# A decode layer, forward and backward: score rows by chunk quarter, outers from score rows, pipelined emission, weights turned on VectorE

## Chip, core and metric

One NeuronCore of a Trainium2 chip runs the whole program. The metric is device time in microseconds (us), lower is better. The kernel before was timed three times on its own: median 883.74 us, from 881.05 to 886.12.

## What is computed

A layer for decoding (two batches, one new token each) and its gradients. Out of the reference:

```python
def _A_ref(x, k_cache, v_cache, wq, wo):          # B=2, Sq=1, D=576, Hq=32, Hkv=16, Sk=4096, Dh=128
    q = (x @ wq).reshape(B, Sq, Hq, Dh).transpose(0, 2, 1, 3)
    k = jnp.repeat(k_cache, 2, axis=1); v = jnp.repeat(v_cache, 2, axis=1)
    p = _softmax(jnp.einsum("bhqd,bhkd->bhqk", q, k) * Dh ** -0.5)
    o = jnp.einsum("bhqk,bhkd->bhqd", p, v)
    return o.transpose(0, 2, 1, 3).reshape(B, Sq, Hq * Dh) @ wo
def _B_ref(x, w_gate, w_up, w_down):              # F=4608
    return jnp.einsum("bsf,fd->bsd", (x @ w_gate) * (x @ w_up), w_down)
out = x + _A_ref(layernorm(x), ...) + _B_ref(layernorm(x), ...)
```

The outputs are this sum and its vector-Jacobian product with grad_out for x, both caches and all five weights. The gradients of the caches have the shape of the caches; each is an outer product of a row over the 4096 tokens with a row of 128. All data are bf16. Reads and writes are about 92.5 MB each, 67.1 MB of each being caches.

## The kernel before

The program is written with a framework that places the semaphores and gives each tile a slot of its tag (`bufs` slots each); it also orders each engine's instructions by readiness and by the order in which they are written, so that later code can run ahead. Each engine runs its own queue in that order. Loads are issued on SyncE's queue, stores on GpSimd's.

There are four groups of four key/value heads (eight query heads each). `group_front` (L322) loads a group's wq and wo, makes q and, with the vector-transposed wo and the stationary Wdy, the gradient of the attention output, and spreads both over partitions (`rep`). `attention` (L377) runs for each batch: GpSimd writes W[0] and W[1], zero-filled stationaries with the query or gradient at eight columns of each 32 (L382), and dM (L386), from which TensorE and ScalarE make BD, block-diagonal rows (L395, L398). Then K scores: each of four heads is loaded as 128 partitions by 32 chunks of 128, turned in 32x32 blocks of bf16 pairs by VectorE (L100 for every vector transpose), and eight matmuls of 512 columns (L414) add into one score tile of 128x1024 fp32. Of its rows, 4 blocks of 32 tokens by 32, only 8 in each 32 hold heads. The softmax over it takes the maximum through TensorE (L467 to L478), the exponential (L481), the sum through TensorE (L484) and the probabilities, which are turned (pT). `token_rows` (L441) turns pT on TensorE into rows by token (L446). The same score code runs on V; then L498 to L511 make the score gradients. `contract` (L424) multiplies with V or K (L430, outputs of 32 partitions in turn); `outer` (L451) makes the 4096x128 gradients by matmuls with 32 rows (L458) into ps_o, a tile of two PSUM banks with two slots, which `evac` (L81) copies out on VectorE (L88) or ScalarE (L91), whichever its running tally finds less loaded. One store of 1 MB follows four evacuations (L462).

`mlp_slice` (L231) handles 512 of the 4608 hidden columns, after each attention and once more at the end: gate and up products with the weights as stationary and two columns moving (L249), the down weights turned on VectorE (L259), the gate/up weights turned on TensorE (`transposed`, L220: L226, L227) and multiplied (L283), rows turned (L291, L296), and outers with two rows (`outer_flat` L201: L212; L308, L315). `group_back` (L522) does the same for wq and wo (L226, L531, L538, L212, L551). The score tile has one slot; caches and weights share ten slots of tag nat, output staging three of tag st.

## Time and profile before

| | |
|---|---|
| median of three runs | 883.74 us |
| the profiled execution, and its span | 885.2 us, 883.4 us |
| TensorE, VectorE, ScalarE, GpSimd busy | 692.2, 390.3, 364.7, 110.1 us |
| mean granted TensorE clock | 0.621 of 2.4 GHz |
| moved by DMA | 185.90 MB, 210 GB/s on average |

The span is the time from the first to the last instruction on the core. A group of instructions is one line, operation and shape; its mean is that of one instruction, and matmuls overlap, so that the busy time divided by the count is often less. The idle time behind the second bar is the time in which the engine stood just before instructions of the group, with what ended it. The DMA share is the mean over the 16 DMA engines. A granted clock of 0.50 is the 1.2 GHz level, 1.00 the 2.4 GHz level; between them is a mixture of both.

### The profile page before, as it was taken

To read this page: it belongs to the slowest core of one execution; us is meant where nothing else is said; L and a number is where in the kernel's file an instruction comes from. 1 tells how busy PE (TensorE), PEld (TensorE's weight loads), DVE (VectorE), ACT (ScalarE), POOL (GpSimd) and SP (SyncE) were. 2 spreads that over 40 slices of the span, in tenths; PEclk is the share of its full clock that TensorE was granted. 3 is DMA by queue.
4 is the path that set the end of the run, shared out by engine and by line. 5 is a ranking of instruction groups with operands and counts; after the bars stand their busy time and mean duration, and the time that the engine had idled before them with its cause. 6 is when DMAs were issued, how large, how long until landed. Compare 5 with 4: busy or idle time off the path is not lost. (4 is left out here: it accounts for less than half of the span.)

```text
span 883.4 us, 14680 instructions
## 1 busy us (share of the span) xinstructions
PE 692.2 (78%) x6469; PEld 338.6 (38%) x6469; DVE 390.3 (44%) x439; ACT 364.7 (41%) x395; POOL 110.1 (12%) x211
## 2 busy tenths in 40 slices
PE   4686878679866897689868687977986689768995
PEld 3244324444333432344424332444433343234552
DVE  8640555145561356244454055514556135624344
ACT  1055425543126531744305551554312653174332
POOL 3010110111201110111111011011120111011111
PEclk9885559555685557755579555855558555775555
DMA  9459623993309850896315972399430985084322
GB/s 338 161 195 401 249 81 115 419 362 136 108 1 391 326 182 25 310 419 247 110 52 185 406 252 81 114 419 363 135 107 1 382 338 180 24 288 185 140 99 89
DMA packets 52368, 185.90 MB, mean 210 GB/s; under 512 B 3880, under 2 KB 18352, under 8 KB 44112
## 3 DMA queue, kind: packets, MB, share of 16 engines
q1 hardware_dynamic: 28064, 92.49, 28.1%
q0 software_dynamic: 24240, 92.48, 27.5%
q8 instruction: 50, 0.82, 0.4%
q14 instruction: 14, 0.11, 0.0%
HBM read 92.48 MB, written 92.48 MB: 209 GB/s over the span
## 5 line engine op out<-in xcount | busy, mean ns | idle before, releaser
L91 ACT CAST so<-ps_o 128x1024 bf16<-128x1024 f32 x221 | 215.9, 1020 | 148.3 <-PE ps_o L458 92.5
L458 PE MATMUL ps_o<-BD,r 32*128 32x512 bf16 x512 | 130.9, 531 | 83.6 <-ACT so L91 49.4
L414 PE MATMUL ps_sc<-X,W 128*128 128x512 bf16 x512 | 170.8, 488 | 15.0 <-POOL W L382 9.7
L100 DVE STREAM_TRANSPOSE X<-kv 128x2048 f32<-128x2048 f32 x64 | 146.8, 2303 | 51.2 <-PE ps_sc L414 51.0
L462 POOL DMA_DIRECT2D out_dram<-so x64 | 48.4, 756 | 409.5 <-ACT so L91 377.4
L414 PEld LDWEIGHTS <-W 128*128 128x128 bf16 x512 | 56.3, 117 | 111.9 <-issue 74.3
L458 PEld LDWEIGHTS <-r 32*128 32x128 bf16 x512 | 27.8, 96 | 126.6 <-issue 97.4
L88 DVE CAST so<-ps_o 128x1024 bf16<-128x1024 f32 x35 | 43.0, 1229 | 27.2 <-PE ps_o L458 17.9
L226 PE MATMUL ps_o<-ident,wgu 128*128 128x128 bf16 x288 | 44.2, 308 | 5.8 <-DVE so L88 4.7
L518 DVE TENSOR_SCALAR oT<-ps_m 128x8 bf16<-128x8 f32 x8 | 1.4, 170 | 104.5 <-PE ps_m L437 104.5
L481 ACT ACTIVATE ex<-ps_sc,negb 128x1024 f32<-128x1024 f32 x8 | 8.9, 1114 | 89.9 <-DVE negb L478 89.9
L430 PE MATMUL ps_m<-kv,dsT 128*32 128x128 bf16 x1024 | 38.9, 267 | 0.9 <-issue 0.9
L91 ACT COPY wT<-ps_o 128x1152 bf16<-128x1152 bf16 x21 | 23.5, 1120 | 35.1 <-PE ps_o L227 35.1
L315 PE MATMUL ps_o<-rows,xn_bf 2*128 2x512 bf16 x72 | 36.5, 614 | 1.0 <-DVE stw L88 0.8
L88 DVE CAST stw<-ps_o 128x1024 bf16<-128x1024 f32 x18 | 21.9, 1218 | 33.8 <-PE ps_o L315 26.1
L91 ACT COPY r<-ps_m 128x1024 bf16<-128x1024 bf16 x16 | 16.5, 1034 | 44.3 <-PE ps_m L446 44.3
L91 ACT CAST stw<-ps_o 128x1024 bf16<-128x1024 f32 x18 | 18.0, 1013 | 37.5 <-PE ps_o L315 37.5
L430 PEld LDWEIGHTS <-dsT 128*32 128x32 bf16 x1024 | 21.5, 111 | 25.8 <-issue 25.8
L226 PEld LDWEIGHTS <-wgu 128*128 128x128 bf16 x288 | 25.9, 136 | 14.1 <-issue 10.5
L91 ACT CAST std<-ps_o 128x1024 bf16<-128x1024 f32 (+1 forms) x27 | 20.7, 801 | 23.2 <-PE ps_o L212 23.1
L100 DVE STREAM_TRANSPOSE Xd<-wd 128x1152 f32<-128x1152 f32 x9 | 12.4, 1377 | 39.9 <-DMA wd<-in_B_w_down_dram 39.9
L382 POOL COPY W<-rep 32x32 bf16<-32x32 bf16 x64 | 13.2, 207 | 104.2 <-PE ps_sc L414 101.4
(165 smaller groups left out, 846.0 us busy)
## 6 DMA issues: line engine op xcount, KB each, us to landing
out_dram<-so POOLq DMA_DIRECT2D x64, 1024.0 KB, 9.8
kv<-in_A_k_cache_dram SPq DMA_DIRECT2D x32, 1024.0 KB, 14.2
kv<-in_A_v_cache_dram SPq DMA_DIRECT2D x32, 1024.0 KB, 8.0
out_dram<-stw POOLq DMA_DIRECT2D x18, 512.0 KB, 3.4
wd<-in_B_w_down_dram SPq DMA_DIRECT2D x9, 576.0 KB, 7.1
out_dram<-std POOLq DMA_DIRECT2D x9, 576.0 KB, 3.1
wo<-in_A_wo_dram SPq DMA_DIRECT2D x4, 1152.0 KB, 19.3
wgu<-in_B_w_gate_dram SPq DMA_DIRECT2D x9, 512.0 KB, 3.8
```

The costliest lines, as they stand in the source:

```text
L88: nc.vector.tensor_copy(out=out, in_=in_)
L91: nc.scalar.copy(out, in_)
L100: nc.vector.transpose(out, in_)
L226: nc.tensor.transpose(tp[:, k - k0, dc * P:(dc + 1) * P], src(k, dc), ident[:])
L315: nc.tensor.matmul(o[:, k, :], lhsT=xn_bf[0:2, (dc + k) * P:(dc + k + 1) * P], rhs=rows[0:2, 1 + w, :], start=True, stop=True)
L382: nc.gpsimd.tensor_copy(view(W[t][:], 32 * a, 32, 32 * a, [[G * P, 4], [P + 2, G], [1, 2]]), view(rep[:], 32 * a, 32, t * 4 * GH * 2 + b, ...
L414: nc.tensor.matmul(s_ps[:, half, :], lhsT=Wt[:, be, l, :], rhs=view(X[:], 0, P, half * 16 * Dh + 64 * (be // 2) + be % 2, [[Dh, 16], [2, 3 ...
L430: nc.tensor.matmul(o_ps[32 * q:32 * q + 32, l, :], lhsT=rowsT[:, c, :], rhs=heads[l][:, c, :], start=(c < 4), stop=(c >= NCH - 4))
L458: nc.tensor.matmul(o[:, q % 2, :], lhsT=r2[32 * q:32 * q + 32, c // 4, :], rhs=bd[32 * q:32 * q + 32].rearrange("p l d -> p (l d)"), start ...
L462: nc.gpsimd.dma_start(oview[b, :, G * g:G * g + G, 8 * Dh * s:8 * Dh * (s + 1)], so[:].rearrange("p l c d -> p l (c d)"))
L481: nc.scalar.activation(ex[:], s_ps[:].rearrange("p a n -> p (a n)"), AF.Exp, bias=negb[:], scale=SCALE, accum_out=z[:])
L518: nc.vector.tensor_scalar(oT[:, 1, :, b], dq_ps[:], SCALE, None, op0=ALU.mult)
```

## The change

- A head's scores take 16 matmuls of 256 columns in place of 8 of 512. W has 24 more columns, and a view shifted by 8 columns puts the chunk quarter cq into the row, so that the score tile is 128x256, with all rows in use and two slots.
- The K/V outers take the score rows themselves (pr, ds) as stationaries; BD gets four copies, each masked on GpSimd to one quarter. `token_rows` is gone. A unit of outers makes two ps_o tiles from four matmuls; a store writes 256 KB of one head and one token block.
- `contract` works per head, with its own evacuation of 128 columns.
- The order is written by hand: `fill` puts two units of outers and some units of the MLP or of the last group's back part (`side`) behind each head's scores.
- wq, gate and up are turned on VectorE (Xq, Xw) and multiplied in `dxn`, which adds into accx; gate and up products have x as stationary and the weights moving. The MLP and group outers take 32-row operands (xnr, dyr, hb, R) in four or two row blocks.
- nat has 11 slots, st 4.

The diff, cut to its core:

```diff
--- before
+++ after
         return ps.tile(list(shape), dtype, tag="m", bufs=2, name="ps_m")
 
     def ps_sc():
-        return ps.tile([P, 2, 512], FP32, tag="sc", bufs=1, name="ps_sc")
-
-    def ps_o(shape=(P, 2, 512), dtype=FP32):
-        return ps.tile(list(shape), dtype, tag="o", bufs=2, name="ps_o")
+        return ps.tile([P, 256], FP32, tag="sc", bufs=2, name="ps_sc")
+
+    def ps_o():
+        return ps.tile([P, 2, 512], FP32, tag="o", bufs=2, name="ps_o")
...
-        return sb.tile(list(shape), BF16, tag="nat", bufs=10, name=name)
+        return sb.tile(list(shape), BF16, tag="nat", bufs=11, name=name)
...
-        return sb.tile(list(shape), BF16, tag="st", bufs=3, name=name)
+        return sb.tile(list(shape), BF16, tag="st", bufs=4, name=name)
...
-    def transposed(src, tail, n, dst):
...
-    def mlp_slice(i):
...
+    def stationaries(rep, half):
+
...
+        nc.vector.tensor_tensor(
+            view(Wm[:], 0, P, 0, [[8, 32], [2, 4], [1, 2]]), view(rep, 0, P, 0, [[2, 32], [0, 4], [1, 2]]),
+            view(mask8[:], 0, P, 0, [[0, 32], [2, 4], [1, 2]]), ALU.mult)
+        for h in range(2):
+            off, dims = half(h)
+            n = len(dims) > 1 and dims[0][1] or 1
+            nc.gpsimd.tensor_copy(
+                view(Wt[:], 64 * h, 64, 0, [[P // n, n], [1, P // n]]), view(Wm[:], 64 * h, 64, off, dims))
...
+    def dxn(Wm, Wt, X, pos, xoff, xstep):
+
+        dp = ps_m([P, 160])
+        for s in range(8):
+            for q in range(4):
+                nc.tensor.matmul(dp[32 * q:32 * q + 32, 0:P], lhsT=view(Wm[:], 0, P, 8 * pos(q, s), [[1, 32]]),
+                                 rhs=view(X[:], 0, P, xoff(q, s), [[xstep, 4], [2, 32]]),
+                                 start=(s == 0), stop=(s == 7))
+        for s in range(4):
+            for q in range(4):
+                nc.tensor.matmul(dp[32 * q:32 * q + 32, P:160], lhsT=view(Wt[:], 0, P, 8 * (4 * q + s), [[1, 32]]),
+                                 rhs=view(X[:], 0, P, 8 * FS + (2 * q + s // 2) * 64 + s % 2, [[2, 32]]),
+                                 start=(s == 0), stop=(s == 3))
+        nc.vector.tensor_add(accx[:], accx[:], dp[:])
...
+        def gate_up():
+            wgu = m["wgu"]
+            ug = ps_m([P, 2, P])
+            for w in range(2):
+                for dc in range(5):
+                    k = 4 * w + dc if dc < 4 else 8
+                    for a in range(4):
+                        nc.tensor.matmul(ug[32 * a:32 * a + 32, 1 - w, :], lhsT=xs[:, dc if dc < 4 else 4 + w, :],
+                                         rhs=wgu[:, k, P * a:P * (a + 1)], start=(dc == 0), stop=(dc == 4))
...
+        def back():
+            wgu = m["wgu"]
+            Xw = xtile([P, 9, FS], "Xw")
+            t32(pairs(Xw[:].rearrange("p c n -> p (c n)")), pairs(wgu[:].rearrange("p c n -> p (c n)")))
...
+        def outer_gu(w):
+            def f():
+                hb = m["hb"]
+                if w == 0:
+                    m["st"] = stile([P, 8, FS], "stw")
+                st = m["st"]
+                o = [ps_o(), ps_o()]
                 for dc in range(4):
+                    for a in range(4):
+                        nc.tensor.matmul(o[a // 2][:, a % 2, dc * P:(dc + 1) * P],
+                                         lhsT=xnr[32 * a:32 * a + 32, dc * P:(dc + 1) * P],
+                                         rhs=hb[32 * a:32 * a + 32, 1 + w, :], start=True, stop=True)
+                for A in range(2):
+                    evac(view(st[:], 0, P, 4 * w * FS + 256 * A, [[P, 2], [FS, 4], [1, P]]),
+                         o[A][:].rearrange("p a (d f) -> p a d f", d=4), 1024)
...
+                for k in range(2):
+                    for aa in range(2):
+                        a = 2 * A + aa
+                        nc.tensor.matmul(o[aa][:, k, 0:HD2], lhsT=R[32 * a:32 * a + 32, 0, h2, :],
+                                         rhs=dyr[32 * a:32 * a + 32, k * HD2:(k + 1) * HD2], start=True, stop=True)
...
+        return [loads, gate_up, down, grads, outer_down(0), outer_down(1), back, outer_gu(0), outer_gu(1), outer_tail]
...
+    okview = out_2.rearrange("b h (a j c4 cb) d -> b h a c4 j (cb d)", a=4, j=32, c4=4)
+    ovview = out_3.rearrange("b h (a j c4 cb) d -> b h a c4 j (cb d)", a=4, j=32, c4=4)
...
+    def build_W(st, b, t):
+        for a in range(4):
+            nc.gpsimd.tensor_copy(
+                view(W[t][:], 32 * a, 32, 24 + 32 * a, [[G * WW, 4], [WW + 2, G], [1, 2]]),
+                view(st["rep"][:], 32 * a, 32, t * 4 * GH * 2 + b, [[GH * 2, 4], [4, G], [2, 2]]),
+            )
+
+    def build_BD(st, b, t):
+
+        nc.gpsimd.tensor_copy(
+            view(dM[:], 0, P, t * G * P, [[P + 2, G], [8, 16], [1, 2]]),
+            view(st["qd"][:], 0, P, (2 if t == 0 else 1) * GH * 2 + b, [[4, G], [0, 16], [2, 2]]),
+        )
+        bp = ps_m([P, G, Dh])
+        for l in range(G):
+            nc.tensor.matmul(bp[:, l, :], lhsT=dM[:, t, l], rhs=ident[:], start=True, stop=True)
+        bd = sb.tile([P, G * Dh], BF16, tag="bd", bufs=2, name="bd")
+        nc.scalar.copy(bd[:], bp[:].rearrange("p l d -> p (l d)"))
+        act(0.6)
+        for c in range(4):
+            nc.gpsimd.tensor_scalar(BD[t][:, c, :], bd[:], maskc[:, c:c + 1], None, op0=ALU.mult)
...
+        for be in range(4):
+            for cq in range(4):
+                nc.tensor.matmul(
+                    s_ps[:], lhsT=view(W[t][:], 0, P, (be * G + l) * WW + 24 - 8 * cq, [[1, P]]),
+                    rhs=view(X[:], 0, P, 2 * cq * Dh + 64 * (be // 2) + be % 2, [[Dh, 2], [8 * Dh, 4], [2, 32]]),
+                    start=(l == 0 and be == 0 and cq == 0), stop=(l == G - 1 and be == 3 and cq == 3),
...
+        o_ps = ps_m([P, Dh])
+        for h in range(2):
+            for c4 in range(4):
+                for cq in range(4):
+                    nc.tensor.matmul(o_ps[32 * cq:32 * cq + 32, :], lhsT=rowsT[:, 4 * h + c4, :],
+                                     rhs=head[:, 8 * c4 + 2 * cq + h, :],
+                                     start=(h == 0 and c4 == 0), stop=(h == 1 and c4 == 3))
+        nc.scalar.copy(o_sb[:, l, :], o_ps[:])
...
+    def outer_units(rows, t, b, g, oview):
+        m = {}
+
+        def unit(A, cq):
+            def f():
+                if cq == 0:
+                    m["st"] = [stile([P, G, 8, Dh], "so") for _ in range(2)]
+                o = [ps_o(), ps_o()]
+                for h in range(2):
+                    for aa in range(2):
+                        a = 2 * A + aa
+                        nc.tensor.matmul(o[aa][:, h, :], lhsT=rows[32 * a:32 * a + 32, P * h:P * (h + 1)],
+                                         rhs=BD[t][32 * a:32 * a + 32, cq, :], start=True, stop=True)
+                for aa in range(2):
+                    evac(m["st"][aa][:, :, 2 * cq:2 * cq + 2, :].rearrange("p l c d -> p c l d"),
+                         o[aa][:].rearrange("p c (l d) -> p c l d", l=G), 1024)
+                if cq == 3:
+                    for aa in range(2):
+                        for l in range(G):
+                            nc.gpsimd.dma_start(oview[b, G * g + l, 2 * A + aa],
+                                                m["st"][aa][:, l].rearrange("p c d -> p (c d)"))
+            return f
+        return [unit(A, cq) for A in range(2) for cq in range(4)]
...
+        def second():
+            Xq = xtile([P, 9, FS], "Xq")
+            t32(pairs(Xq[:].rearrange("p c n -> p (c n)")), pairs(wq[:].rearrange("p c n -> p (c n)")))
...
+        return [first, second, outer_o(0, 0), outer_o(0, 1), outer_o(1, 0), outer_o(1, 1),
+                outer_q(0), outer_q(1), outer_qt]
...
+    side = []
+    outs = []
+
+    def fill(no, ns):
+        for _ in range(min(no, len(outs))):
+            outs.pop(0)()
+        for _ in range(min(ns, len(side))):
+            side.pop(0)()
+
+    side += mlp_units(0)
+    st = group_front(0)
+    for t in range(2):
+        build_W(st, 0, t)
+    build_BD(st, 0, 1)
+    nxt = None
+    for n in range(NIT):
+        g, b = divmod(n, Bq)
+        side += mlp_units(n + 1)
+        per = -(-len(side) // 8)
+        K, V = [], []
+        s_ps = ps_sc()
+        for l in range(G):
+            K.append(head_scores(kview, 0, b, g, l, s_ps))
+            fill(2, per)
+        fill(len(outs), 0)
+        build_BD(st, b, 0)
+        pr, pT = softmax(s_ps)
+        outs += outer_units(pr, 1, b, g, ovview)
+        if b == 1 and g + 1 < NGRP:
+            nxt = group_front(g + 1)
+        if n + 1 < NIT:
+            build_W(st if b == 0 else nxt, (b + 1) % 2, 0)
+        o_sb = sb.tile([P, G, Dh], FP32, tag="o_sb", bufs=2, name="o_sb")
+        dp_ps = ps_sc()
+        for l in range(G):
+            V.append(head_scores(vview, 1, b, g, l, dp_ps))
+            if l > 0:
+                contract(pT, V[l - 1], o_sb, l - 1)
+            fill(2, per)
+        if n + 1 < NIT:
+            build_W(st if b == 0 else nxt, (b + 1) % 2, 1)
+        ds, dsT = dscores(pr, dp_ps)
+        contract(pT, V[G - 1], o_sb, G - 1)
+        t_ps = contract_end(o_sb)
+        nc.vector.tensor_copy(st["oT"][:, 0, :, b], t_ps[:])
+        fill(len(outs), 0)
+        if n + 1 < NIT:
+            build_BD(st if b == 0 else nxt, (b + 1) % 2, 1)
+        o_sb = sb.tile([P, G, Dh], FP32, tag="o_sb", bufs=2, name="o_sb")
+        for l in range(G):
+            contract(dsT, K[l], o_sb, l)
+        t_ps = contract_end(o_sb)
+        nc.vector.tensor_scalar(st["oT"][:, 1, :, b], t_ps[:], SCALE, None, op0=ALU.mult)
+        dve(0.4)
+        outs += outer_units(ds, 0, b, g, okview)
+        if b == 1:
+            side += back_units(st)
+            st = nxt
+    while outs or side:
+        fill(1, 1)
```

## Rows read from the trace of the kernel before

**Rows 1.** Page, part 1: busy us (share) and instructions of each engine.

```profile
PE 692.2 (78%) x6469; PEld 338.6 (38%) x6469; DVE 390.3 (44%) x439; ACT 364.7 (41%) x395; POOL 110.1 (12%) x211
```

**Rows 2.** Busy time by stage: each engine's us (count), clock, DMA share, GB/s.

```profile
0.00:23.00 23.00, 9.10 (x98) 6.99 (x99) 17.79 (x39) 4.00 (x5) 9.29 (x19) 1.00 0.92 341
...
233.00:262.00 29.00, 21.91 (x111) 8.69 (x112) 17.75 (x15) 3.82 (x5) 2.23 (x12) 0.79 0.08 30
...
288.00:320.00 32.00, 28.55 (x224) 14.94 (x223) 14.00 (x16) 18.62 (x20) 3.02 (x4) 0.50 0.80 300
...
372.00:397.00 25.00, 19.17 (x172) 10.43 (x171) 8.53 (x12) 13.28 (x14) 3.02 (x4) 0.50 1.03 419
...
846.00:884.00 38.00, 26.10 (x165) 11.86 (x162) 18.34 (x29) 12.26 (x13) 5.44 (x8) 0.50 0.31 110
```

**Rows 3.** Instruction groups kept: line, shapes, count | busy us, mean ns | idle before, releasers.

```profile
L414 PE MATMUL ps_sc<-X,W 128*128 128x512 bf16 x512 | 170.8, 488 | 15.0 <-POOL W L382 9.7 <-DVE X L100 5.1
...
L458 PE MATMUL ps_o<-BD,r 32*128 32x512 bf16 x512 | 130.9, 531 | 83.6 <-ACT so L91 49.4 <-ACT r L91 17.2 <-DVE so L88 15.7
...
L414 PEld LDWEIGHTS <-W 128*128 128x128 bf16 x512 | 56.3, 117 | 111.9 <-issue 74.3 <-POOL W L382 10.3
...
L430 PE MATMUL ps_m<-kv,dsT 128*32 128x128 bf16 x1024 | 38.9, 267 | 0.9 <-issue 0.9
...
L430 PE MATMUL ps_m<-kv,pT 128*32 128x128 bf16 x1024 | 15.8, 219 | 0.0
```

**Rows 4.** Same view: four of the eighteen TensorE groups that the change deletes.

```profile
L226 PE MATMUL ps_o<-ident,wgu 128*128 128x128 bf16 x288 | 44.2, 308 | 5.8 <-DVE so L88 4.7 <-ACT stqt L91 1.1
...
L315 PE MATMUL ps_o<-rows,xn_bf 2*128 2x512 bf16 x72 | 36.5, 614 | 1.0 <-DVE stw L88 0.8
...
L249 PE MATMUL ps_m<-xnT,wgu 128*128 128x2 bf16 x288 | 21.3, 177 | 0.0
...
L291 PE MATMUL ps_m<-ident,hT 128*2 128x128 bf16 x36 | 5.3, 302 | 0.0
```

**Rows 5.** Same view: TensorE in the softmax.

```profile
L484 PE MATMUL ps_m<-z,Gsum 128*128 128x1 f32 x16 | 4.7, 361 | 11.9 <-ACT ex L481 11.9
...
L476 PE MATMUL ps_m<-one,mr 1*128 1x1 f32 x16 | 4.1, 320 | 19.8 <-DVE mr L474 19.8
...
L469 PE MATMUL ps_m<-identf,mx 128*1 128x128 f32 x8 | 2.2, 270 | 11.0 <-DVE mx L467 11.0
```

**Rows 6.** Same view: evacuations and a vector transpose.

```profile
L91 ACT CAST so<-ps_o 128x1024 bf16<-128x1024 f32 x221 | 215.9, 1020 | 148.3 <-PE ps_o L458 92.5 <-DMA out_dram<-so 51.1 <-ACT o_sb L433 1.0
...
L88 DVE CAST so<-ps_o 128x1024 bf16<-128x1024 f32 x35 | 43.0, 1229 | 27.2 <-PE ps_o L458 17.9 <-DMA out_dram<-so 5.8 <-ACT so L91 3.5
...
L100 DVE STREAM_TRANSPOSE Xo<-wo 128x2304 f32<-128x2304 f32 x4 | 10.3, 2572 | 0.0
```

**Rows 7.** Timeline of TensorE (start us, us, what) in three stretches.

```profile
272.02 0.61 PE L430 MATMUL ps_m<-kv,dsT 128*32 128x128 bf16 x15
272.56 0.61 PE L458 MATMUL ps_o<-BD,r 32*128 32x512 bf16 x2
...
324.80 2.31 PE L414 MATMUL ps_sc<-X,W 128*128 128x512 bf16 x5
...
661.94 1.90 PE L414 MATMUL ps_sc<-X,W 128*128 128x512 bf16 x8 [0.38 <-DVE X L100]
```

**Rows 8.** Instruction groups of GpSimd.

```profile
L462 POOL DMA_DIRECT2D out_dram<-so x64 | 48.4, 756 | 409.5 <-ACT so L91 377.4 <-DVE so L88 17.9 <-issue 14.2
...
L304 POOL DMA_DIRECT2D out_dram<-std x9 | 5.0, 552 | 87.4 <-ACT std L91 87.4
...
L185 POOL MEMSET dM<- 128x1024 bf16 x1 | 0.9, 947 | 0.0
```

**Rows 9.** Page, part 3: DMA queues, packets, MB, share of 16 engines.

```profile
q1 hardware_dynamic: 28064, 92.49, 28.1%
q0 software_dynamic: 24240, 92.48, 27.5%
```

More of the change, by code (lines that the diff above doesn't have):

```diff
@@ new lines @@
+    gp = ps_o()
+    for a in range(4):
+        nc.tensor.matmul(gp[0:2, a // 2, 160 * (a % 2):160 * (a % 2) + 160], lhsT=F8[:, 2 * a:2 * a + 2], rhs=accx[:],
+                         start=True, stop=True)
+    for A in range(2):
+        nc.vector.tensor_copy(view(rowf[:], 0, 2, D + 64 * A, [[32, 2], [P, 4], [1, 32]]),
+                              view(gp[:], 0, 2, 512 * A, [[160, 2], [32, 4], [1, 32]]))
+    t0 = rowf[:, 1, 512:576].rearrange("b (a j) -> b a j", a=2)
+    nc.vector.tensor_copy(t0, view(gp[:], 0, 2, P, [[160, 2], [1, 32]]))
```

620 lines of the change are left out of this document (293 added, 327 removed).

## The prediction

> **What bounds the kernel now.** I read the busy times first. TensorE is busy 692.2 us of 883.4, VectorE and ScalarE 390.3 and 364.7, GpSimd 110.1 [rows 1]; no engine is full. The DMA queues are not full either: their packets took 28.1% and 27.5% of the span [rows 9], about 491 us if they ran without a gap. So I cut the span into stages [rows 2]. Three kinds show. In a score stage (233 to 262) TensorE is busy 21.9 of 29 us and the DMA share is 0.08. While K/V outputs are written (372 to 397) the DMA is full at 419 GB/s. In the MLP stage (288 to 320) TensorE is busy 28.55 of 32 us at a granted clock of 0.50, which is the 1.2 GHz level. Each stage has another limit and little runs beside it: TensorE for most of the time, the DMA for about 25 us of each (group, batch), and TensorE's waits in the softmax.
>
> The groups of TensorE say what its time is. Scores, K/V outers and contractions are 170.8, 130.9 and 38.9 + 15.8 us [rows 3]. Eighteen groups, from 44.2 us (turning gate/up weights) down to 5.3 (turning h rows), are work that the change deletes [rows 4]. The softmax chain adds waits: TensorE stands 11.0 us ahead of the maximum's transpose, 19.8 ahead of L476 and 11.9 ahead of L484 [rows 5], and 17.2 for the copied token rows, which stands in the row of L458 [rows 3].
>
> **What is removed.** The deleted groups are the weight transposes L226 and L227 (44.2 + 19.3 + 17.2 + 7.4), the two-row outers L315, L308, L551 (36.5 + 9.4 + 19.6) and L212 (21.2 + 18.6), the gate/up products L249 (21.3 + 13.8), the row transposes L296, L291, L538 (10.4 + 5.3 + 8.7), the products with turned weights L283 and L531 (13.7 + 6.4), and the token rows L446 (6.8 + 6.2): 286 us of TensorE, of whose 18 rows four are shown [rows 4]. They sit in stages where TensorE is about 89% busy, so I count them on the path in full.
>
> **What is added on TensorE.** A 128-column matmul whose stationary has 32 columns costs 38.9/1024 = 38 ns in a stream [rows 3]; gate_up (40 x 9) and dxn (48 x 13) are of this kind: 984 x 38 ns = 37.4 us. A 32-row matmul of 512 columns costs 130.9/512 = 256 ns, so by columns 64 ns for 128, 128 for 256, 144 for 288: outer_gu and outer_tail (40 x 9) 23.0, outer_down (8 x 9) 10.4, outer_o (16 x 4) 9.2, outer_q and outer_qt (20 x 4) 10.2. The 116 small ones (transposes of R, replications) at about 50 ns make 6. Sum 96 us. From below: half of that, 48, if it all ran at 2.4 GHz. From above: the 1344 matmuls of 128 columns (gate_up, dxn, outer_gu, outer_tail) at the 44.2/288 = 153 ns of L226 [rows 4] make 206 in place of 60, so 242. I take 96, since the nearest rows are those that share the array in the same way.
>
> Scores become 1024 matmuls of 256 columns instead of 512 of 512: the same columns, so 170.8 stays. With the array at 2.4 GHz eight take 1.90 us, 0.238 each; at 1.2 GHz five take 2.31, spaced 0.43 [rows 7]: 122 to 220 us for all. Each is then 0.12 to 0.21 us long beside a weight load of 0.117 [rows 3], which overlaps it; at the high level the two are level, so I add nothing for loads and at most 512 x 0.117 = 60 us if the extra ones stood alone. K/V outers stay 512 matmuls of 512 columns in pairs on two row groups: 130.9. Contractions keep 2048 matmuls: 54.7. TensorE after: 692 - 286 + 96 = 502 us.
>
> The order now alternates full-array, 32-row and 32-column matmuls. The trace already holds this: 15 contractions span 0.61 us and the next pair of outers starts 0.54 after them [rows 7], with no idle between, so I take no cost. At 1.2 GHz two concurrent 512-column matmuls need 0.43, so an alternation costs at most about 0.1 us; with some 500 alternations that is 50 us, kept for the range. The Trainium skill (TensorEngine Tiling (Array Packing), Key Properties) says that changing the tiling mode drains the array. The rows above put a cap on that drain here; by the page alone the sum would only be worse by an amount that it does not state.
>
> **VectorE and ScalarE.** The K/V evacuations stay 256 of 1024 columns, 1020 ns on ScalarE and 1229 on VectorE [rows 6]. ScalarE loses the turned-weight and token-row copies (23.5 + 9.0 + 16.5) and gains small copies (about 10). VectorE loses about 17 (turned weights), 31 (row copies) and 40 (softmax tiles a quarter as wide), and gains 13 transposes of 2304 pairs at 2572 ns [rows 6], 33 us, and about 17 of small work. So about 350 and 325 us: both under 502, hidden if the order lets them.
>
> **GpSimd and the stores.** 64 K/V stores of 1 MB, 756 ns each to issue, become 256 of 256 KB; the cheapest issue is 552 ns [rows 8], so 141 instead of 48 us. The new masks of BD are 64 ops of 512 columns; a memset of 1024 took 947 ns [rows 8], so 0.47 each, at most twice that: 30 to 60. GpSimd ends near 255 us, half of the new time. It runs in order: behind a store that waits for its evacuation stand build_W, build_BD and the next stores, and TensorE's next scores wait for build_W. build_W is emitted half an iteration ahead, so I take 0; uncovered, one store wait of some 3 us per half iteration is 16 x 3 = 48 us. SP's loads keep their number, less the tails.
>
> **Waits.** A second score buffer and the outers of the last iteration stand beside the softmax, so the 42.7 us of its waits and the 17.2 for token rows go: -60. What is late next is TensorE itself, waiting for ps_o: L458 now stands 49.4 for ScalarE and 15.7 for VectorE [rows 3], and that I leave in. Between 0 and 125 of waits can go (also these); I take 60, because the waits for ps_o are in the order of the evacuations, which the change doesn't shorten. Start and end (9.10 of 23 us busy, 26.10 of 38, [rows 2]) I leave: more constants are built (0 to 5 us), and the end trades one serial MLP slice for eight K outers and one group's back units.
>
> Sum, against the profiled execution (885.2 us, span 883.4; 1.5 above the median of 883.74): 885 - 286 + 96 - 60 = **635 us**, so TensorE would be 79% busy, as it is now.
>
> **The rivals.**
> *The DMA and a warm clock.* If TensorE is kept full enough to hold 2.4 GHz, scores fall from 171 to 122 us and TensorE to about 430. Then transfers bind: 491 us of packets, plus an end of some 50 us where nothing is loaded, plus some 15 of start: 560. For it: the clock in score stages is already 0.79. Against: it is 0.50 in the mixed stages [rows 2], and five scores between other matmuls ran at the low level [rows 7].
> *PSUM pairs.* Each outer unit now takes both ps_o buffers, so a unit is two evacuations, 2.04 us on ScalarE, and a refill of about 0.9 (0.61 of matmuls and the signals): some 201 units with 348 evacuations' worth are 355 + 181 = 536 us of one chain. If the 171 of scores stand in that chain instead of beside it, and some 35 of start and end: 740. It decides if units are issued back to back. For it: the row of L458. Against: two units per head stand between scores.
> *The order isn't what is written.* Outers already run between contractions now, and scores between matmuls of the MLP [rows 7], so the instruction order is not the source's order. If the emission order then brings no overlap, only the work goes: 885 - 286 + 96 = 695.
> *Slower: narrow stores.* A K/V store's destination has an outermost dimension of 4, where it was 128. If each store is carried by 4 of the 16 DMA engines, and always the same ones, these carry 67.1 MB of K/V outputs plus a quarter of the other 117.9 MB [rows 9], 96.6 MB at 4 x 419/16 = 105 GB/s: about 922 us, slower than now. It decides at about 4.2 engines: (67.1/n + 7.4) MB at 26.2 GB/s is 885 there; with the stores spread in turn over all 16 it costs nothing. Nothing in the trace shows which engines a store takes. The Trainium skill (DMA: Bandwidth & Descriptors, Why a DMA increments its semaphore by 16 and not by 1) states that the number of engines comes from the slowest dimension of both sides, which here gives 4, and that GpSimd's stores then start from a cursor that moves round; by that the stores would be spread. No run here shows it yet.
>
> **How the numbers follow.** Forecast 635 (own range 580 to 690) 0.48; warm clock 560, 0.18; PSUM pairs 740, 0.14; order without overlap 695, 0.10; narrow stores 922, 0.08; a mixture of small losses that ends about where it is now 0.02. Range 550 to 765: it leaves out the narrow stores, the standstill, and part of the tails of the 560 and 740 cases. From above it holds 695 + 50 (alternations), from below 635 - 65 (waits for ps_o) and the warm case. Faster by over 0.5% 0.90, within 0.5% 0.02, slower 0.08; 0.5% is about what a measurement of this kernel can tell from no change.
>
> **What would show it.** Right: TensorE near 500 us busy and near 80% in every middle stage; no weight transposes; DMA share near 0.7 throughout instead of swinging from 0.08 to 1; no stage in which the softmax leaves TensorE idle for over 2 us. The 560 case: clock near 0.8 and DMA share near 0.9. The 740 case: waits of the outers for ps_o above 150 us. The narrow stores: landing times of tens of us and evacuations waiting for stores. Wrong would make me: added matmuls nearer 153 ns than 38, GpSimd late with W, or a kv buffer that comes free late, since K, wq, wo and the MLP weights hold 8 to 10 of 11 slots and V streams through the rest.

## The result and the profile after

The changed kernel takes 854.3 us (median of four runs, 846.4 to 867.8); the kernel before took 884.0 beside it. The ratio is 0.964, 95% interval 0.956 to 0.971. The forecast was 635, range 550 to 765: the sign was right, the gain an eighth of the forecast's (30 us of 249). The profiled execution took 854.2 us, its span 852.4.

The page of the changed kernel: busy times, DMA packets and queues, and the chain that ended last by engine and by line, each as a share of the span (L487 are the contractions).

```profile
PE 613.6 (72%) x6297; PEld 306.8 (36%) x6297; DVE 355.2 (42%) x436; ACT 325.6 (38%) x436; POOL 357.1 (42%) x508
...
DMA packets 105050, 186.32 MB, mean 219 GB/s; under 512 B 56300, under 2 KB 71288, under 8 KB 96792
...
q0 software_dynamic: 76592, 92.89, 44.0%
q1 hardware_dynamic: 28392, 92.49, 29.5%
...
DMA 45%; PE 27%; POOL 8%; ACT 8%; issue 5%; DVE 4%; SPq 1%; ACTq 0%; POOLq 0%; DVEq 0%
DMA out_dram<-so 41%; PE ps_o L511 8%; PE ps_sc L474 8%; ACT so L93 6%; POOL out_dram L519 6%; PE ps_m L487 3%; POOL BD L461 2%; DMA kv<-in_A_k_cache_dram 2%; DMA out_dram<-sto 1%; PE ps_m L496 1%; DMA wgu<-in_B_w_up_dram 1%; PE ps_o L379 1%; DVE X L102 1%; ACT std L93 1%; PE ps_m L297 1%
```

TensorE lost 79 us of work, not 190 [rows 1], and stands idle for 239 us, where it was 191. GpSimd's queue moves the same bytes in three times as many packets, and these hold the engines half as long again: 44.0% of 852 us, where it was 27.5% of 883 [rows 9]. The chain of waits goes through the landings of K/V stores for 41% of the span.

The costliest groups of the changed kernel (L474 scores, L511 K/V outers, L461 masks of BD, L519 K/V stores; busy, mean ns, idle before):

```profile
L519 POOL DMA_DIRECT2D out_dram<-so x256 | 176.9, 698 | 149.2 <-ACT so L93 76.5
L474 PE MATMUL ps_sc<-X,W 128*128 128x256 bf16 x1024 | 205.9, 349 | 16.2 <-DVE X L102 10.8
...
L511 PE MATMUL ps_o<-BD,pr 32*128 32x512 bf16 x256 | 98.5, 559 | 51.1 <-ACT so L93 47.9
L461 POOL TENSOR_SCALAR BD<-bd,maskc 128x512 bf16<-128x512 bf16 x64 | 99.4, 1559 | 64.8 <-ACT bd L458 61.4
L511 PE MATMUL ps_o<-BD,ds 32*128 32x512 bf16 x256 | 86.7, 499 | 55.2 <-ACT so L93 44.8
```

The kept groups grew: scores from 170.8 to 205.9 us and outers from 130.9 to 185.2, at the same count of columns [rows 3]. All waits of the changed kernel, the four that tell most (us in total, times, longest):

```profile
ACT so L93 <- DMA out_dram<-so: 102.4, 19, 13.4
PE ps_o L511 <- ACT so L93: 92.7, 44, 12.3
...
ACT std L93 <- DMA out_dram<-so: 52.5, 7, 11.4
...
PE ps_o L379 <- ACT std L93: 45.9, 8, 10.8
```

Read downwards this is one queue: a staging tile isn't free because its store has not landed, ScalarE waits, and TensorE waits for ScalarE, even in the MLP's outers (L379), which share the tiles. Issue to landing is 13.8 us for 256 KB, where it was 9.8 for 1 MB. In the packet records a K/V store of the change carries 192 packets of 8 bytes beside its 64 of 4 KB, and a 4 KB packet takes 250 ns on average, where it took 171.

TensorE's timeline of the changed kernel shows why the outers grew (start, us, what). Its granted clock was 0.50 in the first row and 1.00 in the other two:

```profile
300.00 1.03 PE L511 MATMUL ps_o<-BD,pr 32*128 32x512 bf16 x2
...
309.39 0.60 PE L511 MATMUL ps_o<-BD,ds 32*128 32x512 bf16 x4
...
312.11 0.60 PE L511 MATMUL ps_o<-BD,ds 32*128 32x512 bf16 x2
```

Rows may be compared at one level of the clock only. At 0.50 two outers take 1.03 us in the first row, and before the change two took 0.61, also at 0.50 [rows 7]. At 1.00 four take 0.60 us in the second row, and in the third two take as long. So some outers still run two at a time, and others one after the other. Over the whole trace, 267 of the 512 outers started within 0.15 us of the one ahead of them before the change, and 87 do in it (256 would be one in each pair). The clock isn't the cause: at 0.50 an outer cost 293 ns of TensorE's busy time before and 421 now, at 1.00 it was 174 and is 247.

I read the slow pair as both halves (h) of one row block, so the same 32 rows of the array, and the quick one as the two row blocks. The source alternates row blocks, but an outer unit wants two ps_o tiles, and where only one is free the engine would get both halves of the first. The trace doesn't name row blocks; e4 and e11 test the reading. The Trainium skill (TensorEngine Tiling (Array Packing), Key Properties) says that different tiles of the array work independently; the quick rows agree.

### The profile page after: what moved, and what is told of

The parts are those of the page before. It is cut to its first block, busy times and chain, and to the rows that moved or that the text cites. A ratio compares the mean times of both kernels' runs of the same rounds, so it can differ in the third digit from the quotient of the medians.

```text
span 852.4 us, 14847 instructions
## 1 busy us (share of the span) xinstructions
PE 613.6 (72%) x6297; PEld 306.8 (36%) x6297; DVE 355.2 (42%) x436; ACT 325.6 (38%) x436; POOL 357.1 (42%) x508
## 3 DMA queue, kind: packets, MB, share of 16 engines
q1 hardware_dynamic: 28392, 92.49, 29.5%
## 4 chain that ended last, share of the span: by engine, by line
DMA 45%; PE 27%; POOL 8%; ACT 8%; issue 5%; DVE 4%; SPq 1%; ACTq 0%; POOLq 0%; DVEq 0%
DMA out_dram<-so 41%; PE ps_o L511 8%; PE ps_sc L474 8%; ACT so L93 6%; POOL out_dram L519 6%; PE ps_m L487 3%; POOL BD L461 2%; DMA kv<-in_A_k_cache_dram 2%; DMA out_dram<-sto 1%; PE ps_m L496 1%; DMA wgu<-in_B_w_up_dram 1%; PE ps_o L379 1%; DVE X L102 1%; ACT std L93 1%; PE ps_m L297 1%
## 5 line engine op out<-in xcount | busy, mean ns | idle before, releaser
L519 POOL DMA_DIRECT2D out_dram<-so x256 | 176.9, 698 | 149.2 <-ACT so L93 76.5
L474 PE MATMUL ps_sc<-X,W 128*128 128x256 bf16 x1024 | 205.9, 349 | 16.2 <-DVE X L102 10.8
L474 PEld LDWEIGHTS <-W 128*128 128x128 bf16 x1024 | 108.6, 119 | 98.0 <-issue 65.7
L511 PE MATMUL ps_o<-BD,pr 32*128 32x512 bf16 x256 | 98.5, 559 | 51.1 <-ACT so L93 47.9
L461 POOL TENSOR_SCALAR BD<-bd,maskc 128x512 bf16<-128x512 bf16 x64 | 99.4, 1559 | 64.8 <-ACT bd L458 61.4
L511 PE MATMUL ps_o<-BD,ds 32*128 32x512 bf16 x256 | 86.7, 499 | 55.2 <-ACT so L93 44.8
L379 PE MATMUL ps_o<-dyr,hb 32*128 32x288 bf16 x72 | 20.8, 394 | 46.0 <-ACT std L93 45.9
L511 PEld LDWEIGHTS <-ds 32*128 32x128 bf16 x256 | 15.4, 97 | 81.8 <-issue 78.8
L93 ACT CAST stw<-ps_o 128x1024 bf16<-128x1024 f32 x35 | 34.5, 1015 | 22.4 <-PE ps_o L345 20.8
L487 PE MATMUL ps_m<-kv,pT 128*32 128x128 bf16 x1024 | 40.8, 287 | 0.0
L511 PEld LDWEIGHTS <-pr 32*128 32x128 bf16 x256 | 15.5, 101 | 62.9 <-issue 56.0
L487 PEld LDWEIGHTS <-pT 128*32 128x32 bf16 x1024 | 23.5, 120 | 35.6 <-issue 33.9
L487 PE MATMUL ps_m<-kv,dsT 128*32 128x128 bf16 x1024 | 28.9, 283 | 1.9 <-ACT o_sb L490 1.7
L496 PEld LDWEIGHTS ps_m<-R,o_sb 128*128 128x128 f32 x128 | 24.6, 273 | 12.8 <-issue 10.5
L487 PEld LDWEIGHTS <-dsT 128*32 128x32 bf16 x1024 | 22.8, 127 | 17.4 <-issue 16.5
L496 PE MATMUL ps_m<-R,o_sb 128*128 128x2 f32 x128 | 26.9, 318 | 3.0 <-issue 3.0
## 6 DMA issues: line engine op xcount, KB each, us to landing
out_dram<-so POOLq DMA_DIRECT2D x256, 256.0 KB, 13.8
```

Of the source, the lines that this page charges most:

```text
L93: nc.scalar.copy(out, in_)
L379: nc.tensor.matmul(o[aa][:, k, 0:HD2], lhsT=hb[32 * a:32 * a + 32, 0, :], rhs=dyr[32 * a:32 * a + 32, k * HD2:(k + 1) * HD2], start=True, ...
L461: nc.gpsimd.tensor_scalar(BD[t][:, c, :], bd[:], maskc[:, c:c + 1], None, op0=ALU.mult)
L474: nc.tensor.matmul(s_ps[:], lhsT=view(W[t][:], 0, P, (be * G + l) * WW + 24 - 8 * cq, [[1, P]]), rhs=view(X[:], 0, P, 2 * cq * Dh + 64 * ( ...
L487: nc.tensor.matmul(o_ps[32 * cq:32 * cq + 32, :], lhsT=rowsT[:, 4 * h + c4, :], rhs=head[:, 8 * c4 + 2 * cq + h, :], start=(h == 0 and c4 ...
L496: nc.tensor.matmul(t_ps[:, 2 * l:2 * l + 2], lhsT=o_sb[:, l, :], rhs=R40[:, 2 * l:2 * l + 2], start=True, stop=True)
```

## Experiments

The first theory was that narrow stores take the gain; the rivals were GpSimd's masks, the wait for two ps_o tiles, and TensorE itself.

**Wide stores by another column order (e1, e2).** The columns of the scores are reordered so that a store covers 128 adjacent partitions; e2 also merges four stores into one of 1 MB.

```diff
-rhs=view(X[:], ..., [[Dh, 2], [8 * Dh, 4], [2, 32]])
+rhs=view(X[:], ..., [[Dh, 2], [2, 32], [8 * Dh, 4]])
-okview = out_2.rearrange("b h (a j c4 cb) d -> b h a c4 j (cb d)", ...)
+okview = out_2.rearrange("b h (a p cb) d -> b h a p (cb d)", a=4, p=P)
```

> Only the order of a score block's 128 columns changes (token index outside, chunk quarter inside), so that each of the 256 K/V stores writes 128 consecutive rows of 2 KB: its outermost dimension is 128 instead of 4. Same bytes, same number of stores, same matmuls. Theory of narrow stores (each store carried by few DMA engines, landing late, staging tiles free late): the 49152 packets of 8 B vanish, the store packets of 4 KB fall from 250 to about 171 ns, queue 0 from 44% to about 30%, landing from 13.8 to under 9 us, and the time to 720 to 770 us. Theory of a late GpSimd (masks of 1.56 us, 256 issues of 0.70): not the store's shape but its issue is late, so 835 to 855. Theory of PSUM pairs: 835 to 855.

> As e1_wide, and one store of 1 MB per token block in place of four of 256 KB: 64 issues in place of 256. Theory of narrow stores: within 15 us of e1_wide, since the issues are beside the chain. Theory of a late GpSimd: 130 us of issue time go from GpSimd (177 to about 48), so 30 to 80 us below e1_wide. Theory of PSUM pairs: no change against e1_wide.

Measured: 996.8 us (ratio 1.129, 1.125 to 1.134) and 995.9 (1.128, 1.124 to 1.133). The page of e1 (busy, clock by slices, scores, stores with their landing):

```profile
PE 932.6 (94%) x6297; PEld 321.4 (32%) x6297; DVE 360.0 (36%) x436; ACT 328.5 (33%) x436; POOL 316.5 (32%) x508
...
PEclk9855555555555555555555555555555555555555
...
L474 PE MATMUL ps_sc<-X,W 128*128 128x256 bf16 x1024 | 479.1, 611 | 5.4 <-DVE rz L543 5.0
...
out_dram<-so POOLq DMA_DIRECT2D x256, 256.0 KB, 4.1
```

On the stores the theory held: no 8-byte packets, 178 ns for 4 KB, landing after 4.1 us. But the edit itself cost more than it gave: 468 ns for each score matmul instead of 201, since the moving operand now steps 2048 bytes from column to column instead of 4. The lower clock of e1 is not the reason: in unbroken runs its scores start 437 ns apart at both levels of the granted clock, the change's 213 ns apart at 1.2 GHz and 111 at 2.4. The time of e1 says nothing on what cheap stores are worth.

**Masks on VectorE, and one ps_o per row block (e3, e4).** Both are made on the changed kernel with its own stores.

```diff
-nc.gpsimd.tensor_scalar(BD[t][:, c, :], bd[:], maskc[:, c:c + 1], ...)
+nc.vector.tensor_scalar(BD[t][:, c, :], bd[:], maskc[:, c:c + 1], ...)
```
```diff
-o = [ps_o(), ps_o()]; for h: for aa: matmul(o[aa][:, h, :], ...); for aa: evac
+for aa: o = ps_o(); for h: matmul(o[:, h, :], ...); evac
```

> Only the four masked copies of BD (64 instructions of 1.56 us) move from GpSimd to VectorE. Theory of a late GpSimd: 99 us leave its queue and BD is there earlier, so 780 to 815 us. Theory of narrow stores: 840 to 855, the chain still held by landings. Theory of PSUM pairs: 840 to 855.

> Only the K/V outers: a unit takes one ps_o tile, fills it with two matmuls and copies it out, then the next, in place of both tiles at once. Consecutive matmuls are then on the same row group. Theory of PSUM pairs: the waits of the outers for ps_o (92.7 us) fall by half and the time by 30 to 60 us, to 795 to 825. Theories of narrow stores and of a late GpSimd: 840 to 870, with the outers' busy time higher since pairs no longer share the array.

Measured: 848.1 us (815 to 853, too wide a spread for a ratio) and 855.1 (0.972, 0.965 to 0.979). GpSimd had 99 us less to do in e3, and the chain still went through K/V stores for 43% of the span; in e4 for 35%. The wait for two ps_o tiles doesn't hold the kernel. On the masks e3 leaves it open: three of its runs took 843 to 853 us, one took 815, near the upper end of what a late GpSimd would give. In e4 the two halves of a row block always follow each other, and L511 is 191 us, nearly the change's 185; 76 of its outers start within 0.15 us of the one ahead, 87 in the change. So in the change the halves mostly followed each other already.

**Cheap stores at no other cost (e7).** Each store takes one slice of 32 partitions and its four heads.

```diff
-for l in range(G):
-    dma_start(oview[b, G*g + l, 2*A + aa], m["st"][aa][:, l])
+for c4 in range(4):
+    dma_start(oview[b, 2*A + aa, c4, :, G*g:G*g + G], m["st"][aa][32*c4:32*c4 + 32])
```

> Scores as in the changed kernel. Only the four stores of a staging tile are cut another way: each takes one slice of 32 partitions for all four heads (outermost dimension 32) in place of one head over four times 32 rows (outermost dimension 4). Same 256 stores of 256 KB, same 2 KB runs. Theory of narrow stores: the 8 B packets vanish, landing falls under 9 us, ScalarE no longer waits 100 us and more for stores, and the time is 700 to 780 us. Theory that staging is slow only because stores are many, or that TensorE's order sets the time anyway: 835 to 860.

Measured: 829.6 us (0.936, 0.933 to 0.940). Its page:

```profile
PE 640.1 (77%) x6297; PEld 308.1 (37%) x6297; DVE 354.0 (43%) x436; ACT 325.3 (39%) x436; POOL 320.6 (39%) x508
...
q0 software_dynamic: 27440, 92.49, 36.5%
...
L511 PE MATMUL ps_o<-BD,ds 32*128 32x512 bf16 x256 | 109.3, 579 | 25.2 <-ACT so L93 13.4
L511 PE MATMUL ps_o<-BD,pr 32*128 32x512 bf16 x256 | 108.1, 562 | 21.5 <-ACT so L93 17.4
...
out_dram<-so POOLq DMA_DIRECT2D x256, 256.0 KB, 5.5
```

The 8-byte packets are gone and stores land after 5.5 us. The outers' wait for ScalarE falls from 92.7 to 30.8 us, though VectorE still stands 48.7 us for staging tiles. (The chain of e7 could be followed over only some 17% of the span, so its shares are not set beside the 41%.) So the narrow stores were on the path, and yet worth only 25 us: the outers now take 217 us, with 42 of them close behind another, TensorE is busy 640 us instead of 614, and its own time comes next. Why still fewer of them pair, no run separated.

**Wide stores by remapped tokens (e8, e9).** Tokens are laid out at the load (four loads of 2 KB runs for a head), so that a store is 1 MB over 128 partitions; e9 adds the masks on VectorE.

```diff
-dma_start(n, src[b, G*g + l])
+for a in range(4): dma_start(n[32*a:32*a + 32], src[b, G*g + l, a])   # 2 KB runs
```

> Tokens are spread over partitions and chunks in another way at the load (four loads of 256 KB per head, each 32 partitions by four runs of 2 KB), so that with unchanged scores a token block's store is 128 consecutive rows of 2 KB per head: 64 stores of 1 MB. Theory of narrow stores: like e7_slices or up to 40 us better, because the issue on GpSimd falls from 177 to about 50 us; 690 to 770 us. If the loads now suffer, queue 1 rises above 30% and the time is above that of e7_slices.

> As e8_remap, with the masked copies of BD on VectorE as well. If GpSimd becomes the next bound once stores are wide: 20 to 50 us below e8_remap. If TensorE and its waits for evacuations are next: within 10 us of e8_remap.

Measured: 870.6 us (0.984, 0.979 to 0.989) and 871.4 (0.985, 0.983 to 0.986). Stores are cheap (177 ns for 4 KB), but the load queue goes from 29.5% to 44.0%: the cost moved to the loads. The masks make no difference here.

**The narrow stores in the old order (e10).** The kernel before, with its K/V loads and stores split like the change's stores.

```diff
-oview: "b h (p c) d -> b p h (c d)"           # one store of 1 MB
+oview: "b h (j c4 c) d -> b h c4 j (c d)"     # four stores, outermost dimension 4; loads as 4 x 32 partitions
```

> The kernel before with only its loads and K/V stores changed: partitions hold the tokens in another order (four loads of 32 partitions per head), so that each store of one head writes an outermost dimension of 4 by 32 rows of 2 KB, 256 stores of 256 KB. Theory of narrow stores: the store packets of 4 KB rise from 171 to about 250 ns, 8 B packets appear, and each of the 16 stretches in which K/V outputs are written, full at 419 GB/s before, takes some 8 us more: 960 to 1030 us. If narrow stores cost nothing by themselves: 880 to 900.

Measured: 1061 us (1040 to 1074, too wide a spread for a ratio) against 884.4. The page of e10, packets and the end of the chain:

```profile
DMA packets 107669, 186.37 MB, mean 179 GB/s; under 512 B 59176, under 2 KB 73648, under 8 KB 99408
...
DMA out_dram<-so 19%; PE ps_sc L415 12%; PE ps_o L226 4%; PE ps_o L459 4%; ACT so L91 3%; PE ps_m L431 3%; DMA kv<-in_A_v_cache_dram 3%; PE ps_o L212 3%; DVE X L100 3%; DMA kv<-in_A_k_cache_dram 3%; POOL out_dram L464 2%; DMA wd<-in_B_w_down_dram 2%; PE ps_m L249 2%; PE ps_m L259 2%; PE ps_m L438 2%
```

In the old order, where outputs come in bursts, the same stores (with slower loads: 496 ns instead of 331 for 8 KB) cost 156 to 190 us. Spread over the iteration, as the change spreads them, they cost 25. The loads' part of it was not separated, so that the bursts are the cause is my reading and not shown.

**Paired outers (e11, e12, e14, e15).** One ps_o tile holds both row blocks of one half, so that the pair is always issued together; one staging tile of 16 KB takes its evacuation. Its room comes from load slots: 9 in place of 11 in e11; e12 is the control with 9 slots and no pairs.

```diff
-o = [ps_o(), ps_o()]
-for h: for aa: matmul(o[aa][:, h, :], ...)      # then one evac for each aa
+for h:
+    o = ps_o()
+    for aa: matmul(o[:, aa, :], ...)
+    evac(m["st"][:, :, :, 2*cq + h, :], o)      # st: [P, 2, G, 8, Dh]
```

> Edit, from the kernel with sliced stores (each K/V store one 32-partition slice of four heads): both row blocks (aa = 0, 1) of a K/V outer go into the two halves of one ps_o tile and one 16 KB staging tile, so that the two matmuls on different row groups are always issued next to each other and one evacuation of 1024 columns follows; two such tiles, two 8 KB tiles for the other stores, 9 slots for loads in place of 11. Theory (TensorE's own time in its order is the bound, and the outers grew because the same row group follows itself): L511 falls from 217 us to 130 to 150 us, TensorE from 640 to about 560, the time from 830 to 750 to 780. Rival 1 (evacuations and stores set the pace of the outers): L511 falls as well, but the idle time of TensorE takes it up, and the time stays at 815 to 835. Rival 2 (the outers are long because of the clock, not of their order): L511 stays above 190 us, the time at 820 to 840.

> Edit, from the kernel with sliced stores: 9 slots for loads in place of 11, nothing else. It is there to price what the kernel with paired outers gives up for its staging tiles. If slots don't bind: 826 to 838 us, TensorE still 640 busy. If they bind (loads of wq, wo and the MLP weights then stand behind K and V): 860 or more, with waits of VectorE's transposes for loads.

Measured: e11 835.4 us (0.944, 0.939 to 0.948), e12 864.3 (0.977, 0.974 to 0.980). L511 fell to 140 us and TensorE to 574.7, as expected, but 9 slots cost 35 us, so pairing gave 29 us for 74 less of TensorE's work. Busy times of e11 and of its control e12, and two rows of TensorE, one of e11 and one of e7, both at a granted clock of 0.50:

```profile
PE 574.7 (69%) x6297; PEld 304.7 (37%) x6297; DVE 360.3 (44%) x436; ACT 322.6 (39%) x436; POOL 318.2 (38%) x508
...
PE 648.3 (75%) x6297; PEld 312.8 (36%) x6297; DVE 356.6 (41%) x436; ACT 325.5 (38%) x436; POOL 320.4 (37%) x508
...
345.64 0.61 PE L511 MATMUL ps_o<-BD,ds 32*128 32x512 bf16 x2 [1.43 <-ACT so L93]
...
351.52 1.01 PE L511 MATMUL ps_o<-BD,pr 32*128 32x512 bf16 x2 [0.23 <-ACT so L93]
```

Two outers take 0.61 us again, as before the change. In e11 252 of the 512 start within 0.15 us of the one ahead, in e12 43; at a granted clock of 0.50 one costs 294 ns in e11, 455 in e12 and 293 before the change. So it is the order that made the outers dear. All waits of e11:

```profile
PE ps_sc L474 <- DVE X L102: 84.5, 35, 9.9
...
DVE X L102 <- DMA kv<-in_A_v_cache_dram: 63.4, 10, 11.2
DVE X L102 <- DMA kv<-in_A_k_cache_dram: 54.4, 14, 13.6
```

TensorE waits for transposes, and these for loads, for want of a slot if I read it rightly. With a tenth slot, from single buffers for four small tiles (e14), and with the masks moved as well (e15):

> Edit, from the kernel with paired outers: 10 slots for loads instead of 9; the room comes from single buffers for four small tiles (o_sb, bd, stt, mr). The paired outers took 74 us of TensorE time out and 29 us of the run, against the same 9 slots without pairs; TensorE then stood 84.5 us for VectorE's transposes, and these 118 us for loads. Theory (late loads took the rest): the waits of VectorE for loads fall below 90 us, L511 stays at 140 us, the time 790 to 815. Rival (the single buffers or the order of the evacuations bind now): 825 to 845, with waits of ScalarE and GpSimd for bd or o_sb above those of the run before.

> Edit, from the kernel with paired outers and 10 slots: the masks of BD on VectorE instead of GpSimd, 64 operations. Theory (GpSimd isn't the limit even with cheap stores): within 1% of the run with the masks on GpSimd, GpSimd about 220 us busy. Rival (BD, single-buffered bd and the stores queued behind the masks hold the outers up): 10 to 25 us faster.

Measured: e14 **774.4 us (0.877, 0.872 to 0.882)**, e15 782.9 (0.886, 0.880 to 0.892). Page and waits of e14, and its last stretch (us, busy and count of PE, PEld, DVE, ACT, POOL, clock, DMA share, GB/s):

```profile
PE 585.9 (75%) x6297; PEld 311.8 (40%) x6297; DVE 359.9 (46%) x436; ACT 323.1 (42%) x436; POOL 318.2 (41%) x508
...
L474 PE MATMUL ps_sc<-X,W 128*128 128x256 bf16 x1024 | 208.9, 360 | 45.8 <-DVE X L102 42.8
...
L511 PE MATMUL ps_o<-BD,ds 32*128 32x512 bf16 x256 | 73.5, 568 | 24.6 <-ACT so L93 14.1
L511 PE MATMUL ps_o<-BD,pr 32*128 32x512 bf16 x256 | 68.3, 559 | 13.3 <-ACT so L93 10.7
...
DVE X L102 <- DMA kv<-in_A_v_cache_dram: 34.4, 8, 10.2
...
730.00:780.00 50.00, 19.66 (x93) 4.93 (x93) 19.27 (x28) 16.12 (x19) 16.39 (x30) 0.50 0.61 180
```

e14 came in below the 790 us expected; VectorE stands 47 us for K/V loads, where it stood 118 in e11. Against e7, which has 11 slots, TensorE has 54 us less to do and the run is 55 us shorter, with 193 us idle in place of 190: with loads in time the work comes off the time one for one. The masks on VectorE gain nothing (e15 is 1.1% slower), so GpSimd isn't the limit here.

**The emission order (e13).** From e7, outers are emitted where they are created.

```diff
 outs += outer_units(...)
+fill(len(outs), 0)
```

> Edit, from the kernel with sliced stores: the K/V outers are emitted where they are created, as in the kernel before, instead of two per head between the next scores. Theory (the pipelining is worth its waits): the softmax stands bare again and the outers run against their evacuations, so 30 to 60 us more: 860 to 890; scores run in denser stretches, so the granted clock there rises and L474 falls from 201 to 170 to 185 us. Rival (spreading the outers costs in clock what it gains in waits): 820 to 840, L474 below 180. Second rival (the instruction order is the scheduler's, whatever is emitted): same time and same L474 within 1%.

Measured: 874.9 us (0.989, 0.984 to 0.994), TensorE 665.0 busy, scores 222.0. The pipelining is worth 45 us, but not as I thought: in the profiled runs TensorE's idle time differs by 14 us (204 to 190) and its busy time by 25, of which scores are 21. I had expected the scores to get cheaper in denser stretches; they got dearer. In e13 253 of the 1024 score matmuls start at the 2.4 GHz level, in e7 435, at much the same price for each level (146 and 135 ns of busy time at 2.4 GHz, 240 and 241 at 1.2).

**The width of the scores (e17).** The kernel before, each score matmul split into two of 256 columns.

```diff
-matmul(s_ps[:, half, :], lhsT=Wt, rhs=view(X, ..., [[Dh, 16], [2, 32]]))
+for q in range(2): matmul(s_ps[:, half, 256*q:256*q + 256], lhsT=Wt, rhs=view(X, ..., [[Dh, 8], [2, 32]]))
```

> Edit, from the kernel before the change: each score matmul of 512 columns becomes two of 256, with the same stationary and the same columns; nothing else. It settles why the scores' group grew from 171 to over 200 us. Theory (it is the clock and the mixing in the new order, not the width): L414 stays at 168 to 180 us, the time within 1% of 884. Rival (a 256-column matmul costs more per column, or the extra weight loads stand alone): L414 at 195 us or more, the time 895 to 915.

Measured: 887.7 us (1.003, 1.001 to 1.005). Its group on the page:

```profile
L415 PE MATMUL ps_sc<-X,W 128*128 128x256 bf16 x1024 | 173.4, 336 | 14.5 <-POOL W L382 9.7
```

173.4 for 170.8: the width, and twice the weight loads, cost 2.6 us. The rest of the growth by 35 comes from where the scores stand; the next section takes it apart.

**Do the costs hide one another? (e18 to e20)** e18 is e14 with the change's own stores. e19 is e14 with 11 slots, one 8 KB staging tile instead of two and a single hb; e20 has 11 slots and one K/V staging tile instead of two.

```diff
-nat bufs=10; so2 bufs=2; st bufs=2
+nat bufs=11; so2 bufs=2; st bufs=1    # e19
+nat bufs=11; so2 bufs=1; st bufs=2    # e20, with e11's double buffers for small tiles
```

> Edit, from the changed kernel: paired outers, 10 slots and the four single buffers as in the version of 774 us, but with the change's own K/V stores (outermost dimension 4). With TensorE's outers serial the narrow stores cost 854 - 830 = 25 us. Theory (the two costs hide each other; with TensorE short the stores are the bound): 830 to 850, so that the stores are worth 55 to 75 us here and the pairs nearly nothing without them; the chain goes through the landings of K/V stores. Rival (the costs add): 774 + 25 = 790 to 805.

> Edit, from the version of 774 us (paired outers, sliced stores, 10 slots): the eleventh slot back; its room comes from a single 8 KB staging tile for the stores other than K/V (in place of two) and a single hb. Theory (slots are still what TensorE waits for): the waits of VectorE for K/V loads fall from some 70 to under 30 us and the time to 745 to 765. Rival (with 10 slots loads come early enough, and the single staging tile makes the MLP's outers wait for stores of 7 to 8 us): 775 to 800.

> Edit, from the version with paired outers and 9 slots: 11 slots, and one 16 KB staging tile for the K/V outers instead of two. If slots are what counts and the wait for one store's landing (5 to 6 us, 32 times, partly beside scores) is hidden: 760 to 780. If the landings stand in the path: 830 to 900, with ScalarE and VectorE waiting for K/V stores more than 100 us.

Measured: e18 808.9 us (0.916, 0.914 to 0.919), e19 822.1 (0.933, 0.927 to 0.938), e20 981.3 (1.109, 1.105 to 1.113). With narrow stores pairing is worth 45 us, with cheap ones 55; narrow stores cost 25 us without pairs and 35 with them. That lies between the two expectations, near the second: the costs nearly add. All waits of e18:

```profile
DVE X L102 <- DMA kv<-in_A_k_cache_dram: 111.7, 13, 13.3
ACT so L93 <- DMA out_dram<-so: 87.1, 15, 14.2
```

The price of narrow stores is paid by loads too: K loads land after 12.9 us instead of 8.9 in e14. In e19 VectorE's waits for K/V loads fell to 24 us, as expected, and yet the kernel is 48 us slower than e14, more than the rival had it. GpSimd stands 56.9 us for ScalarE's evacuations of stw, and TensorE 59.2 us for transposes, where it stood 42.8; which of the two single buffers, the staging tile or hb, costs the time was not separated. Here the two were worth more than a load slot. e20, with a single K/V tile, is about 200 us slower than e14, beyond the 900 us of its second case; ScalarE stands 132.8 us for K/V stores.

## Why the prediction was wrong

Between the 854 us and the 635 lie 219: 111.4 of TensorE's work and 107.6 of its idle time, in the profiled run.

**What was removed** was right: the eighteen groups are gone. That all 286 us stood on the path no run tests by itself. **What was added** was 105 us for the 90 priced group by group: gate_up and dxn 34 for 37, outer_gu and its tail 24 for 23, outer_q 11 for 10; the 288-column outers missed by a factor of two and 1.6 (outer_down 20.8 for 10.4, outer_o 15.1 for 9.2). They take two ps_o tiles in the same way as L511, so I think that they lose the same concurrency; no run changed their order.

**TensorE after, 502 us: the step that failed most.** It was 613.6. "K/V outers stay 130.9" took the trace's price of a pair and left open whether the new unit keeps pairs. I saw that a unit takes two ps_o tiles and priced it as a wait (the rival of 740), but not as an order that puts the same rows behind each other: 54 us busy, 86 in e7. Shown by e11 and e14 against e12 and e7; worth 55 us of time. "Scores stay 170.8" missed by 35 us, of which the width has 2.6 (e17). Sorting the 1024 score matmuls by the granted clock at their start takes the rest apart. In e17, 560 start at the 2.4 GHz level and cost 119 ns of busy time each, 464 at 1.2 GHz and cost 230. In the change it is 454 at 141 ns and 570 at 249. At e17's prices the change's mixture of levels makes 185 us, 12 more than e17's 173.4. The other 21 are dearer matmuls at the same level. In unbroken runs they start as far apart as in e17 (213 ns at 1.2 GHz, 110 and 111 at 2.4), but the change has the scores in 196 runs between other matmuls, e17 in 62. About 9 of the 21 us are overlap with a neighbouring group, counted in both. Contractions, kept at 54.7, took 69.7.

**Waits, minus 60: failed.** The named waits of the softmax went, but idle time rose from 191 to 239 us, and in e14 it is still 193. What came instead is in the rows: landings of stores (the outers stand 92.7 us for ScalarE, where they stood 49.4), transposes behind loads (42.8 us in e14, 5.1 before), and the end. From 800 us on, the change has 15.44 us of TensorE in 52.4, and e14's last stretch 19.66:

```profile
800.00:852.40 52.40, 15.44 (x61) 3.96 (x60) 17.04 (x26) 9.87 (x12) 14.47 (x21) 0.53 0.54 126
```

What is pipelined past the last scores stands alone there. I had left start and end as they were.

**Narrow stores: priced as all or nothing.** The rival of 922 asked whether always the same four engines serve a store, and got 0.08; between that and "costs nothing" I had no case. What happened is between: 0.15 us more to issue (698 to 546 ns in e1), 192 tiny packets, 250 for 171 ns, a landing over three times as late as e1's, a chain that goes through these landings for 41% of the span, and 25 us. The Trainium skill (DMA: Bandwidth & Descriptors, Why a DMA increments its semaphore by 16 and not by 1) has four engines and a moving start; the 854 us, below the 922 worked out for it, speak against all stores sharing the same four, and which engines a store took no row shows.

**GpSimd** was 357 for 255 us: masks 1559 ns for the 470 to 940 I bounded from a memset, and the issues above. With cheap stores that cost nothing (e9, e15); beside the narrow ones e3 leaves it open. **The alternation**, taken as free with 0.1 us each kept for the range, is seen in the scores: some 12 us of them, net of overlap, for 134 more runs, about 0.09 us each. For the other groups it was not counted. **The warm clock** did not come: the mean granted clock is 0.641, where it was 0.621. **Load slots**, which I named as what would make me wrong, do bind, once slots are taken away (e12).

From 854 to 635: stores 25 us and serial outers 55 (net of the slot that e14 gives up), shown by runs, lead to e14's 774 (its profiled run 780.4). The other 145 of that run are TensorE 586 for 502 (scores 38, outers 11, contractions 8, the rest 27) and idle 193 for 131, of which start and end are some 24; beyond that no run settles them.

## What to carry to other kernels

Price a kept group again when its order changes: a concurrent pair is a property of what is issued next to each other, and a PSUM tile that holds both members keeps them together whatever comes free first. Look at a store's partition pattern before its bytes, and try a longer outermost dimension (here 32 in place of 4, by slicing the staging tile, without touching the data layout). Compare two rows of TensorE only where the granted clock is the same. When work comes off the busiest engine, look at what feeds it: here one slot for loads decided whether 74 us less work were worth 29 us (9 slots), or 54 us less were worth 55 (10 slots, against 11 without pairs).

## What was not expected of the hardware

- A moving operand with an inner step of 2048 bytes costs 468 ns of busy time for 256 columns, where a step of 4 bytes costs 201 (e1, the change). In unbroken runs the first start 437 ns apart at 1.2 and at 2.4 GHz alike. TensorE was 94% busy in e1 and its granted clock at 5 tenths in 38 of 40 slices.
- GpSimd takes 1559 ns to scale 128x512 bf16 by a scalar of each partition.
- A store of 256 KB with an outermost dimension of 4, 32 or 128 landed after 13.8, 5.5 and 4.1 us (medians, the change, e7, e1; what else was moving differs between the three).
